# Conv ahead of the carried products, one ring of 4 KB tiles, and stores behind the loads, in a retention layer with a gated unit

## The chip, the core and the metric

The kernel runs on one core of a Trainium2 chip. The metric is device time in microseconds (us), from one launch of the whole kernel. TensorE (PE) does the matrix products and writes PSUM; VectorE (DVE), ScalarE (ACT) and GpSimd (POOL) do the elementwise work; SyncE (SP) issues nearly all DMAs. Each engine runs its own instructions in the order in which they were issued to it, and they wait for each other by semaphores.

## What is computed

Multi-head retention (causal, with a decay per head), its heads put side by side as `x`, then a gated unit: a causal convolution of 5 taps per channel through a sigmoid, times a product of `x` with a matrix, times another matrix. Cut to what matters:

```python
batch, n_heads, seq, head_dim = (8, 8, 576, 64)      # d_model 512, all float32

scores = scale * np.matmul(q, k.transpose(0, 1, 3, 2))
Dmat = np.where(rel >= 0, gamma[:, None, None] ** rel[None, :, :], 0.0)
x = np.matmul(scores * Dmat[None], v)                 # then heads side by side: (8, 576, 512)

for k in range(5):
    gate_pre += conv_w[k][None, None, :] * xp[:, k:k + S, :]
gate = 1.0 / (1.0 + np.exp(-gate_pre))
out = gate * (x @ w_val) @ w_out
```

## The kernel before, in words

**Units.** The sequence of each of the 8 batches is cut into two chunks of 256 positions and a tail of 64. A full unit is one chunk of one batch (units 0 to 15; an even unit is the first chunk of its batch, an odd one the second). Units 16 and 17 are the tails of four batches each. Within a unit two blocks of 128 positions are worked on side by side.

**Steps of a unit.** `load_half` brings half of the heads of k, q or v into a float32 tile of 2 KB per partition (`load1` brings all heads at once for the units in `whole`). Where it is given an engine as `touch`, that engine writes one element of the tile first, so that the load is not issued before that point of the engine's order. `cast_half` and `cast1` make bf16 of them, most on GpSimd; v is scaled by the decay on the way. `turn_bank` transposes half of k and q on TensorE into PSUM and copies it out on ScalarE (`kq`, L320). `scores` multiplies q and k, `masks` puts the causal mask on it on VectorE (L361, L365). `update` multiplies k and v for the running state and copies it to `xf` on ScalarE (L470); `states` sums it on GpSimd into `s1` and `s2` (L484 to L496). `carried(u, odd)` multiplies q with the state of the blocks before: the first thing in an output bank. It needs `s1` of its own unit and, for an odd unit, `s2` of the unit before. `values` adds the masked scores times v to the same bank. `fence` and `fence_first` read one element of the bank, so that what comes next into it waits for the first products there. `take_x` scales the bank and writes it to `xg` on VectorE (L436; L443 for tails).

**Steps of a job.** A job is one or two units of the gated unit. `conv` does the five taps as products with diagonal blocks (PSUM tile `a`) and ScalarE makes the gate from it (L542). `value` multiplies `xg` with the value weights, `gated` multiplies with the gate on VectorE (L565), `project` multiplies with the output weights, and ScalarE copies the result to `ob` (L580). `store` sends it out from SyncE.

**Tiles.** Units 0, 1, 16 and 17 are loaded whole into tiles of 4 KB with two buffers for each of k, q, v; the output weights have four constant tiles `wof`; the outputs have three buffers `ob` of 4 KB. PSUM: tile `a` (one buffer of two banks), `s` (the same), `o0` and `o1`, and two of `v`.

**Order.** The whole order is written out by hand (the tile scheduler is set to manual): a first phase for units 0 to 3 with their jobs (L619 to L774), a loop `for n in range(4, NU - 2)` (n = 4 to 15), and an end for units 16 and 17 (L813 to L854). The loop runs several things at once: carried, scores(n,1) and values of unit n; scores(n+1,0) and update of n+1; transposes of n+1 and n+2; loads of n+2 and n+3; casts of n+2 and n+3; conv, gate and gated product of an earlier job; project and store of unit n-3. `fill` adds small products with zeros until a count of products has a certain remainder. In n = 4 and 5 conv works on one of the older, half-wide jobs.

The loop's order, by its lines: carried and scores(n,1) (L782, L783), masks, fence on ScalarE (L785), conv (L786), the second half of k of n+2 (L787), scores(n+1,0) (L788), values(n,0), update with the states (L791), q (L792), values(n,1), first transposes (L795), gated products and loads of n+3 (L796 to L801), casts on GpSimd (L802 to L807), second transposes (L808), project and store (L810 to L812).

Of the kernel before, what the change touches and what calls it, by code (L numbers as in the profile page):

```python
# [13 lines left out]
F32 = mybir.dt.float32  # L14
# [7 lines left out]
def kernel(  # L22
# [10 lines left out]
    nc = tc.nc  # L33
# [8 lines left out]
    GB = 4  # L42
# [38 lines left out]
    with tc.manual_schedule():  # L81

        loaded = {}
        SRC = {"k": k, "q": q, "v": v}

        whole = (0, 1, NU - 2, NU - 1)
        HH = H // 2

        def load1(n, u, touch=None):
            kind, b, c = units[u]  # L90
            src = SRC[n]
            if u in whole:
                t = ldp.tile([P, H, 2 * D], F32, name=f"w{n}c")
                if touch:
                    touch(t[0:1, 0, 0:1], lsc[0:1])
                if kind == "full":
                    nc.sync.dma_start(out=t, in_=src[b, :, c * W:(c + 1) * W, :].rearrange("h (p r) d -> p h (r d)", r=2))
                else:
                    for i in range(GB):
                        nc.sync.dma_start(out=t[i * 32:(i + 1) * 32],  # L100
                                          in_=src[b + i, :, NC2 * W:S, :].rearrange("h (p r) d -> p h (r d)", r=2))
                loaded[n, u] = [(t, 0, H)]
            else:
                for i in range(2):
                    load_half(n, u, i)

        def load_half(n, u, i, touch=None):
            if u in whole:
                if i == 0:
                    load1(n, u, touch)  # L110
                return
            kind, b, c = units[u]
            t = ldp.tile([P, HH, 2 * D], F32, name=f"f{n}{i}")
            if touch:
                touch(t[0:1, 0, 0:1], lsc[0:1])  # L115
            nc.sync.dma_start(out=t, in_=SRC[n][b, i * HH:(i + 1) * HH, c * W:(c + 1) * W, :].rearrange("h (p r) d -> p h (r d)", r=2))
            loaded.setdefault((n, u), []).append((t, i * HH, HH))

        def load(u):
# [5 lines left out]
        cwn = consts.tile([KC * NP, P], F32, name="cwn")  # L125
        nc.scalar.dma_start(out=cwn, in_=moe_conv_w.rearrange("k (o i) -> (k o) i", i=P))
        wvf = [None] * NP
        wof = [consts.tile([P, DM], F32, name=f"wof{o}") for o in range(NP)]
        load(1)


# [4 lines left out]
            nc.sync.dma_start(out=wvf[g], in_=moe_w_val[:, g * P:(g + 1) * P].rearrange("(o i) j -> i o j", i=P))  # L136

        def load_wo(o, touch=None):
            if touch:
                touch(wof[o][0:1, 0:1], lsc[0:1])  # L140
            blk = 2 * (o % 2) + o // 2
            nc.sync.dma_start(out=wof[o], in_=moe_w_out[blk * P:(blk + 1) * P, :])
# [11 lines left out]

        def fill():
            z = ps_v.tile([P, 512], F32, name="v")
            while (made[0] + 32 + 16 + 16) % BLOCK != PLACE:
                matmul(z[:, 0:64], lhsT=zero[:, 0:P], rhs=zero[:, 0:64], start=True, stop=True)

        zero = consts.tile([P, 512], BF16, name="zero")  # L160
# [138 lines left out]
        def new_turned(u):  # L299
            if u not in kqt:  # L300
                kqt[u] = [tp_sb.tile([P, 2, 2, 2, 2, 64], BF16, name=f"kq{hf}") for hf in range(2)]
# [11 lines left out]
        def turn_bank(u, hf, ps):  # L313
            for i in range(2):
                for prl in range(2):
                    for r in range(2):
                        h = 2 * (2 * hf + prl)
                        transpose(ps[:, i, prl, r, :], bf[u]["kq"[i]][:, r, h:h + 2, :].rearrange("p h d -> p (h d)"), ident)
            new_turned(u)
            nc.scalar.copy(kqt[u][hf].rearrange("p i l r c a -> p (i l r c a)"), ps.rearrange("p i l r a -> p (i l r a)"))  # L320

        def turn_halves(*pairs, pool=None):
            if len(pairs) == 1 and pool is None:
                turn_bank(*pairs[0], ps_v.tile([P, 2, 2, 2, P], BF16, name="v"))
            else:
                ps = ps_a.tile([P, 2, 2, 2, 2, P], BF16, name="a")
                for (at, pair) in enumerate(pairs):
                    turn_bank(*pair, ps[:, at])

        def take_part(u, i, eng):  # L330
            for hf in range(2):
# [146 lines left out]

        def states(u):
            kind, b, cu = units[u]  # L480
            xf = xfs[u]
            s1 = stp.tile([P, NP, 64], BF16, name="s1")
            if cu == 0:
                nc.gpsimd.tensor_copy(s1, xf[:, 0])  # L484
                run = stp.tile([P, NP, 64], F32, name="run")
                nc.gpsimd.tensor_tensor(run, xf[:, 0], xf[:, 1], op=ALU.add)
                s2 = stp.tile([P, NP, 64], BF16, name="s2")
                nc.gpsimd.tensor_copy(s2, run)
                state[b, 0] = None
                state[b, "run"] = run  # L490
            else:
                mid = stp.tile([P, NP, 64], F32, name="mid")
                nc.gpsimd.tensor_tensor(mid, state[b, "run"], xf[:, 0], op=ALU.add)
                nc.gpsimd.tensor_copy(s1, mid)
                s2 = stp.tile([P, NP, 64], BF16, name=f"s4{b}", bufs=1)
                nc.gpsimd.tensor_tensor(s2, mid, xf[:, 1], op=ALU.add)  # L496
            state[b, 2 * cu + 1] = s1
            state[b, 2 * cu + 2] = s2
# [70 lines left out]
        def project(j, m, r, split=0, eng=None, pool=None):  # L569
            u = jobs[j][m]  # L570
            o = (pool or ps_v).tile([P, DM], F32, name="v" if pool is None else "s" if pool is ps_s else "o0")
            for jj in range(NP):
                z = zsb[j][:, jj, m * W:(m + 1) * W].rearrange("p (a r) -> p r a", r=2)
                n = DM // 2 if jj < split else DM
                for c in range(0, DM, n):
                    matmul(o[:, c:c + n], lhsT=z[:, r, :], rhs=wob[:, jj, c:c + n], start=(jj == 0 and c == 0),
                                     stop=(jj == NP - 1), skip_group_check=True)
            if r == 0:
                outs[u] = op_sb.tile([P, 2, DM], F32, name="ob")
            (eng or nc.scalar.copy)(outs[u][:, r], o)  # L580

        def last_rows(j):
# [9 lines left out]
            for r in range(2):  # L592
                (act, dve)[r](ob[r], o[r])  # L593
                for i in range(GB):
                    (nc.sync, nc.scalar)[i % 2].dma_start(out=out[b + i, NC2 * W:S, :].rearrange("(p r) n -> r p n", r=2)[r],
                                                          in_=ob[r][i * 32:(i + 1) * 32])

        def store(u):
            kind, b, c = units[u]
# [148 lines left out]
        carried(3, 0)  # L748
        scores(3, 1, lambda: carried(3, 1), pool=ps_a)
        masks(3, 1)  # L750
        load_half("k", 6, 0, dve)
        load_half("q", 6, 0)
        project(0, 0, 0)
        project(0, 0, 1)
        store(0)
        turn_halves((4, 0))
        values(3, 1)
        values(3, 0)
        cast_half("k", 5, 0)
        cast_half("q", 5, 0)  # L760
        fill()
        update(4)
        take_x(3)
        load_half("v", 6, 0, dve)
        turn_halves((4, 1), (5, 0))
        scores(4, 0)
        masks(4, 0)
        prep_tail_mask()
        cast1("v", 5)
        cast_half("k", 5, 1)  # L770
        cast_half("q", 5, 1)
        cast_half("k", 6, 0)
        cast_half("q", 6, 0)
        load_half("v", 6, 1)  # L774
        for n in range(4, NU - 2):
            def bring(name, u, i, eng):
                if u < NU:
                    load_half(name, u, i, eng)

            j, i = (HALVED, n - 4) if n < 6 else place[n - 2 - n % 2][0:1] + (n % 2,)  # L780
            jp, mp = place[n - 3]
            carried(n, 0)  # L782
            scores(n, 1, lambda: carried(n, 1))  # L783
            masks(n, 1)
            fence_first(n, act)  # L785
            conv(j, i)  # L786
            bring("k", n + 2, 1, act)  # L787
            scores(n + 1, 0, pool=ps_v)  # L788
            masks(n + 1, 0)
            values(n, 0)  # L790
            update(n + 1)  # L791
            bring("q", n + 2, 1, act)  # L792
            values(n, 1)
            turns = ps_a.tile([P, 2, 2, 2, 2, P], BF16, name="a")
            turn_bank(n + 1, 1, turns[:, 0])  # L795
# [6 lines left out]
            cast1("v", n + 2)  # L802
            cast_half("k", n + 2, 1)
            cast_half("q", n + 2, 1)
            if n + 3 < NU:
                cast_half("k", n + 3, 0)
                cast_half("q", n + 3, 0)  # L807
# [1 line left out]
            bring("v", n + 3, 1, act)  # L809
            project(jp, mp, 0)  # L810
            project(jp, mp, 1)
            store(n - 3)  # L812
        n = NU - 2  # L813
        j = place[n - 1][0]

        def rows_out(u, pools):
            for r in range(2):
                project(*place[u], r, pool=pools[r])
            store(u)

        carried(n, 0)
        scores(n, 1, lambda: carried(n, 1))
# [12 lines left out]
        scores(n + 1, 1, lambda: carried(n + 1, 1), pool=ps_a)  # L835
        masks(n + 1, 1)
        conv(j, 1, pool=ps_s)
        values(n + 1, 1)
        values(n + 1, 0)
        take_x(n + 1)  # L840
        value(j, 1, 0)
        value(j, 1, 1)
        conv(LAST - 1, 0)
        gated(j, 1, 0)
        gated(j, 1, 1)
        rows_out(n - 2, (ps_s, ps_o))
        gate_values(LAST - 1, 0, 0)
        gate_values(LAST - 1, 0, 1)
        conv(LAST, 0)
# [35 lines left out]
```

## Time and profile before

| | |
|---|---|
| median of 3 runs | 167.01 us (165.39 to 170.68) |
| the profiled execution | 166.65 us, span 164.9 us |
| granted TensorE clock, mean | 0.987 |
| busy: PE, DVE, ACT, POOL | 144.5, 104.9, 97.7, 104.2 us |
| moved by DMA | 40.32 MB: 30.42 read from HBM, 9.44 written to it |
| busy share of the DMA engines by stretches of 10 us, from 50 to 130 | 0.87 to 0.96 |
| the same from 130 to 140, 140 to 150 | 0.28, 0.13 |

The profile is of one execution. Its span runs from the first instruction to the last; what the time has beyond it lies around the program. A group or a line gives an engine, the line of the kernel (a helper's line, L150, for all matrix products), output and input tile, how many instructions, and how long. What stands in square brackets is how long the engine was idle ahead of it and what ended that. "SPq" is the DMA queue of SyncE; "us to landing" runs from the issue of a DMA to its last byte. The clock is the share of full speed that TensorE was granted.

By the granted clock and the chain of waits, the kernel has a first phase to about 41 us, the loop to about 133 us, and an end.

### The profile page before, as it was taken

Reading aid. Unit: us, or ns where it says so; the run is one execution under the profiler, and the core shown is the slowest. Engines: PE = TensorE matmul, PEld = TensorE weight load, DVE = VectorE, ACT = ScalarE, POOL = GpSimd, SP = SyncE. Lnnn points to the kernel's source line nnn. Section 1 sums busy time; section 2 is a strip of 40 time slices with the busy share of each in tenths; the row PEclk is TensorE's granted clock in tenths of the full one; section 3 lists DMA queues with packets and bytes.
Section 4 is the critical chain, followed back from the end, with each engine's and each line's share of the span. In section 5 each row is a group of like instructions: output and inputs, shape, how many; then the busy total and the mean of one; then the engine's idle time right before and its main releaser. Section 6 shows DMA issues by size and latency. Waiting matters only on the chain.

```text
span 164.9 us, 7223 instructions
## 1 busy us (share of the span) xinstructions
PE 144.5 (88%) x3038; PEld 99.6 (60%) x3058; DVE 104.9 (64%) x219; ACT 97.7 (59%) x176; POOL 104.2 (63%) x164
## 2 busy tenths in 40 slices
PE   6987899994998989999999999999987799799970
PEld 2456678873966757575866767575746455457530
DVE  5886877774658666676676768676666538633130
ACT  6894685975475756666666567666554264313620
POOL 7677869698797957979788887878276370000000
PEclk9999999999599999999999999999999999999999
DMA  4999999999779997999999898998898830303254
GB/s 131 347 346 343 322 303 319 323 280 341 217 214 302 279 299 208 310 281 289 292 274 309 245 323 231 319 274 279 218 286 237 251 132 10 131 0 127 109 161 115
DMA packets 62750, 40.32 MB, mean 244 GB/s; under 512 B 2410, under 2 KB 59774, under 8 KB 62718
## 3 DMA queue, kind: packets, MB, share of 16 engines
q1 hardware_dynamic: 62496, 39.59, 78.5%
q8 instruction: 24, 0.39, 1.0%
q10 hardware_dynamic: 222, 0.27, 0.6%
q14 instruction: 8, 0.07, 0.1%
HBM read 30.42 MB, written 9.44 MB: 242 GB/s over the span
## 4 chain that ended last, share of the span: by engine, by line
PE 54%; ACT 6%; DMA 6%; DVE 4%; issue 2%; SPq 1%; POOL 0%; ACTq 0%; POOLq 0%
PE v L150 25%; PE a L150 18%; PE o L150 6%; PE s L150 5%; ACT gate L542 5%; DMA out_dram<-ob 3%; DMA wqc<-in_q_dram 3%; DVE p L365 2%; ACT kq L320 1%; DVE xg L443 1%; SPq L100 1%; DVE p L361 1%; DVE last L593 0%; POOL qb L278 0%; ACTq L542 0%
## 5 line engine op out<-in xcount | busy, mean ns | idle before, releaser
L320 ACT COPY kq<-a 128x1024 bf16<-128x1024 bf16 x27 | 27.3, 1013 | 22.0 <-PE a L150 20.3
L150 PE MATMUL v<-xg,wvb 128*128 128x256 bf16 (+1 forms) x180 | 34.2, 322 | 1.9 <-DVE xg L443 1.2
L365 DVE TENSOR_TENSOR p<-s,mask 128x1024 bf16<-128x1024 f32 x17 | 20.8, 1223 | 15.5 <-PE s L150 15.5
L271 POOL TENSOR_TENSOR vb<-fv,gin 128x512 bf16<-128x512 f32 x28 | 28.7, 1044 | 1.1 <-PE a L150 0.9
L542 ACT ACTIVATE gate<-a 128x1024 f32<-128x1024 f32 (+1 forms) x17 | 16.6, 974 | 21.4 <-PE a L150 21.4
L565 DVE TENSOR_TENSOR zz<-gate,v 128x512 bf16<-128x512 f32 x24 | 16.5, 688 | 15.7 <-PE v L150 14.0
L150 PEld LDWEIGHTS <-wvb 128*128 128x128 bf16 x192 | 17.7, 97 | 12.5 <-issue 1.9
L150 PE MATMUL a<-xg,dg 64*64 64x256 bf16 (+1 forms) x460 | 23.7, 326 | 0.5 <-DVE xg L436 0.3
L436 DVE TENSOR_TENSOR xg<-o,gout 128x512 bf16<-128x512 f32 x32 | 22.2, 733 | 2.5 <-PE o L150 2.4
L150 PEld LDWEIGHTS <-kb 64*64 64x64 bf16 (+1 forms) x656 | 16.4, 108 | 11.8 <-issue 4.6
L278 POOL CAST kb<-fk 128x512 bf16<-128x512 f32 x28 | 17.1, 614 | 5.8 <-DMA fk<-in_k_dram 4.8
L150 PEld LDWEIGHTS <-kq 64*64 64x64 bf16 x576 | 17.1, 107 | 3.3 <-issue 2.7
L150 PE MATMUL v<-wob,zz 128*128 128x512 bf16 x79 | 18.8, 379 | 0.1
L150 PEld LDWEIGHTS <-dg 64*64 64x64 bf16 x480 | 17.3, 107 | 2.0 <-issue 1.2
L580 ACT COPY ob<-v 128x512 f32<-128x512 f32 x28 | 16.3, 582 | 2.2 <-PE v L150 1.3
L150 PE MATMUL o<-p,vb 64*64 64x128 bf16 x576 | 16.1, 222 | 1.1 <-DVE p L365 0.6
L361 DVE TENSOR_TENSOR p<-v,mask 128x512 bf16<-128x512 f32 x24 | 15.4, 685 | 0.8
L278 POOL CAST qb<-fq 128x512 bf16<-128x512 f32 x22 | 13.5, 616 | 3.3 <-DMA fq<-in_q_dram 1.6
L150 PE MATMUL a<-ident,kb 128*128 128x128 bf16 x108 | 10.7, 222 | 4.9 <-ACT gate L542 2.2
L150 PEld LDWEIGHTS <-zz 128*128 128x128 bf16 x96 | 8.8, 98 | 8.9 <-DVE fq L115 0.5
L150 PEld LDWEIGHTS <-vb 64*64 64x64 bf16 x576 | 11.8, 108 | 2.7 <-issue 2.2
L150 PE MATMUL s<-kq 64*64 64x128 bf16 x304 | 11.7, 222 | 1.5 <-DVE p L365 1.1
(111 smaller groups left out, 223.8 us busy)
## 6 DMA issues: line engine op xcount, KB each, us to landing
out_dram<-ob SPq DMA_DIRECT2D x16, 512.0 KB, 5.0
fk<-in_k_dram SPq DMA_DIRECT2D x28, 256.0 KB, 4.3
fq<-in_q_dram SPq DMA_DIRECT2D x28, 256.0 KB, 4.5
fv<-in_v_dram SPq DMA_DIRECT2D x28, 256.0 KB, 4.5
wkc<-in_k_dram SPq DMA_DIRECT2D x2, 512.0 KB, 4.9
wqc<-in_q_dram SPq DMA_DIRECT2D x2, 512.0 KB, 5.4
wvc<-in_v_dram SPq DMA_DIRECT2D x2, 512.0 KB, 5.9
wof<-in_moe_w_out_dram SPq DMA_DIRECT2D x4, 256.0 KB, 4.7
```

Of the source, the lines that this page charges most:

```text
L100: nc.sync.dma_start(out=t[i * 32:(i + 1) * 32], in_=src[b + i, :, NC2 * W:S, :].rearrange("h (p r) d -> p h (r d)", r=2))
L150: return f(*a, **k)
L271: nc.gpsimd.tensor_tensor(b[n][:, hs].rearrange("p h r d -> p (h r) d"), f.rearrange("p h (r d) -> p (h r) d", r=2), gin[:, units[u][2], h ...
L278: (eng or nc.gpsimd.tensor_copy)(b[n][:, :, hs].rearrange("p r h d -> p h r d"), f.rearrange("p h (r d) -> p h r d", r=2))
L320: nc.scalar.copy(kqt[u][hf].rearrange("p i l r c a -> p (i l r c a)"), ps.rearrange("p i l r a -> p (i l r a)"))
L361: nc.vector.tensor_tensor(p[:, par].rearrange("p l r a -> p l (r a)"), sps[u, hf][par].rearrange("p l r a -> p l (r a)"), mrow.to_broadcas ...
L365: nc.vector.tensor_tensor(p.rearrange("p e l r a -> p (e l) (r a)"), sps[u, hf].rearrange("p e l r a -> p (e l) (r a)"), mrow.to_broadcast ...
L436: nc.vector.tensor_tensor(x[:, b, :, PAD + i0:PAD + i0 + P].rearrange("p o (a r) -> p o r a", r=2), o[c].rearrange("p o (r a) -> p o r a", ...
L443: nc.vector.tensor_tensor(x[:, b + 2 * c + i, :, PAD + i0:PAD + S].rearrange("p o (a r) -> p o r a", r=2), o[c].rearrange("p o (r a) -> p ...
L542: nc.scalar.activation(t, cps[j, i], AF.Sigmoid)
L565: nc.vector.tensor_tensor(zsb[j][:, 2 * e + ss[0]:2 * e + ss[-1] + 1, :], gsb[j, i][e], vps[j, i, e], op=ALU.mult)
L580: (eng or nc.scalar.copy)(outs[u][:, r], o)
```

## The change

- `big()` gives tiles of 4 KB from one ring of eleven. Whole loads (units 0 and 1 only), pairs of output weights, and the outputs come from it in this order. Units 16 and 17 are loaded in halves, so each half is four DMAs of 64 KB where a whole load was four of 128 KB.
- `turn_halves` transposes all its pairs, then copies them out.
- In the loop conv comes ahead of carried (but in n = 4 behind it); the fence goes from ScalarE to VectorE; update comes ahead of values(n,0); the states of n+1 are made on GpSimd behind the casts of v, k and q of n+2. scores(n,1) no longer has a part of carried between its products.
- Outputs are put on a list. One store is issued at the end of each odd n, and the others by twos behind the loop.
- The entry of the loop and the end have a new order.

```diff
+        def big():
+            return ldp.tile([P, 2, DM], F32, name="big", bufs=11)
...
-        whole = (0, 1, NU - 2, NU - 1)
+        whole = (0, 1)
...
-                t = ldp.tile([P, H, 2 * D], F32, name=f"w{n}c")
...
+                t = big().rearrange("p c (h d) -> p (c h) d", d=2 * D)
+                nc.sync.dma_start(out=t, in_=src[b, :, c * W:(c + 1) * W, :].rearrange("h (p r) d -> p h (r d)", r=2))
...
+            hs = slice(i * HH, (i + 1) * HH)
+            if kind == "full":
+                nc.sync.dma_start(out=t, in_=SRC[n][b, hs, c * W:(c + 1) * W, :].rearrange("h (p r) d -> p h (r d)", r=2))
+            else:
+                for g in range(GB):
+                    nc.sync.dma_start(out=t[g * 32:(g + 1) * 32],
+                                      in_=SRC[n][b + g, hs, NC2 * W:S, :].rearrange("h (p r) d -> p h (r d)", r=2))
...
-        wof = [consts.tile([P, DM], F32, name=f"wof{o}") for o in range(NP)]
+        wof = [None] * NP
...
         def load_wo(o, touch=None):
+            if wof[o] is None:
+                t = big()
+                for c in range(2):
+                    wof[o // 2 * 2 + c] = t[:, c]
...
-            while (made[0] + 32 + 16 + 16) % BLOCK != PLACE:
+            while (made[0] + 32 + 16 + 8) % BLOCK != PLACE:
...
                 for (at, pair) in enumerate(pairs):
-                    turn_bank(*pair, ps[:, at])
+                    turn_bank(*pair, ps[:, at], take=False)
+                for (at, pair) in enumerate(pairs):
+                    take_bank(*pair, ps[:, at])
...
-                outs[u] = op_sb.tile([P, 2, DM], F32, name="ob")
+                outs[u] = big()
...
+        waiting = []
+
+        def stores(n):
+            for u in waiting[:n]:
+                store(u)
+            del waiting[:n]
...
         masks(3, 1)
+        prep_tail_mask()
...
-        store(0)
-        turn_halves((4, 0))
+        waiting.append(0)
+        turn_halves((4, 0), (4, 1))
...
         fill()
-        update(4)
+        update(4, now=False)
         take_x(3)
         load_half("v", 6, 0, dve)
-        turn_halves((4, 1), (5, 0))
-        scores(4, 0)
-        masks(4, 0)
-        prep_tail_mask()
         cast1("v", 5)
         cast_half("k", 5, 1)
         cast_half("q", 5, 1)
+        scores(4, 0, pool=ps_v)
+        masks(4, 0)
+        turn_halves((5, 0), pool=ps_a)
+        load_half("v", 6, 1, act)
+        states(4)
         cast_half("k", 6, 0)
         cast_half("q", 6, 0)
-        load_half("v", 6, 1)
+        def carry(n):
+            carried(n, 0)
+            carried(n, 1)
...
-            carried(n, 0)
-            scores(n, 1, lambda: carried(n, 1))
+            scores(n, 1)
             masks(n, 1)
-            fence_first(n, act)
+            if n == 4:
+                carry(n)
             conv(j, i)
+            if n > 4:
+                carry(n)
+            fence_first(n, dve)
             bring("k", n + 2, 1, act)
             scores(n + 1, 0, pool=ps_v)
             masks(n + 1, 0)
+            update(n + 1, now=False)
+            bring("q", n + 2, 1, act)
             values(n, 0)
-            update(n + 1)
-            bring("q", n + 2, 1, act)
             values(n, 1)
...
             cast1("v", n + 2)
             cast_half("k", n + 2, 1)
             cast_half("q", n + 2, 1)
+            states(n + 1)
             if n + 3 < NU:
                 cast_half("k", n + 3, 0)
                 cast_half("q", n + 3, 0)
...
-            store(n - 3)
+            waiting.append(n - 3)
+            if n % 2:
+                stores(1)
         n = NU - 2
+        stores(2)
...
-            store(u)
+            waiting.append(u)
+            stores(2)
...
         conv(j, 1, pool=ps_s)
+        value(j, 1, 0)
         values(n + 1, 1)
         values(n + 1, 0)
-        take_x(n + 1)
-        value(j, 1, 0)
+        gated(j, 1, 0)
         value(j, 1, 1)
         conv(LAST - 1, 0)
-        gated(j, 1, 0)
         gated(j, 1, 1)
-        rows_out(n - 2, (ps_s, ps_o))
+        take_x(n + 1)
+        stores(2)
+        rows_out(n - 2, (ps_s, None))
```

More of the change, by code (lines that the diff above doesn't have):

```diff
@@ L92, in load1 @@
             if u in whole:
-                t = ldp.tile([P, H, 2 * D], F32, name=f"w{n}c")
[L94 to L101, printed above, removed]
+                t = big().rearrange("p c (h d) -> p (c h) d", d=2 * D)
+                nc.sync.dma_start(out=t, in_=src[b, :, c * W:(c + 1) * W, :].rearrange("h (p r) d -> p h (r d)", r=2))
                 loaded[n, u] = [(t, 0, H)]
@@ L115, in load_half @@
                 touch(t[0:1, 0, 0:1], lsc[0:1])
-            nc.sync.dma_start(out=t, in_=SRC[n][b, i * HH:(i + 1) * HH, c * W:(c + 1) * W, :].rearrange("h (p r) d -> p h (r d)", r=2))
+            hs = slice(i * HH, (i + 1) * HH)
[5 more added lines that the diff above has]
+                                      in_=SRC[n][b + g, hs, NC2 * W:S, :].rearrange("h (p r) d -> p h (r d)", r=2))
             loaded.setdefault((n, u), []).append((t, i * HH, HH))
@@ L311, in turn, with turn_bank @@
                         transpose(ps[:, hf, prl, r, :], bf[u]["kq"[i]][:, r, h:h + 2, :].rearrange("p h d -> p (h d)"), ident)
-        def turn_bank(u, hf, ps):
+        def turn_bank(u, hf, ps, take=True):
             for i in range(2):
@@ L318, in turn_bank, with take_bank @@
                         transpose(ps[:, i, prl, r, :], bf[u]["kq"[i]][:, r, h:h + 2, :].rearrange("p h d -> p (h d)"), ident)
+            if take:
+                take_bank(u, hf, ps)
+        def take_bank(u, hf, ps):
             new_turned(u)
@@ L480, in states @@
             kind, b, cu = units[u]
+            if kind != "full":
+                return
             xf = xfs[u]
```

## The prediction

> **What bounds the kernel now.** I read the page first: TensorE is busy 88% of the span, no other engine above 64%, DMA at 0.9 and more through the middle. Next the chain of waits in order of time. One iteration of the steady loop (n = 10) and the start of the next:
>
> ```profile
> 87.46 1.03 ACT gate L542
> 88.54 0.61 PE a L150 x8
> 89.15 0.22 PE v L150
> 89.41 1.46 PE v L150 x6
> 90.87 0.45 PE a L150 x8
> 91.32 1.73 PE v L150 x8
> 93.05 0.24 PE o L150 x4
> ...
> 93.84 1.12 PE a L150 x17
> 95.03 1.03 ACT gate L542
> ```
>
> Columns are start, duration, what. The loop is TensorE all round, except one hop: conv ends, ScalarE makes the gate for 1.03, and the transposes into the same PSUM tile wait for it. Call G the start of a gate. G is 56.99, 65.14, 72.51, 80.09, 87.46, 95.03, 102.40, 109.98, 117.35, 125.93, 135.44 for n = 6 to 16: 7.38 where the unit has one carried state, 7.57 where it has two; 8.15, 8.58 and 9.51 once each.
>
> Then the timeline of GpSimd in the same iteration, and the DMA issues:
>
> ```profile
> 89.11 0.72 POOL L493 TENSOR_TENSOR mid<-run,xf 128x256 f32<-128x256 f32 x1 [0.28 <-ACT xf L470]
> 89.90 0.40 POOL L494 CAST s<-mid 128x256 bf16<-128x256 f32 x1
> 90.26 0.73 POOL L496 TENSOR_TENSOR s<-mid,xf 128x256 bf16<-128x256 f32 x1
> 90.94 2.05 POOL L271 TENSOR_TENSOR vb<-fv,gin 128x512 bf16<-128x512 f32 x2
> 92.93 0.62 POOL L278 CAST kb<-fk 128x512 bf16<-128x512 f32 x1
> 93.53 0.62 POOL L278 CAST qb<-fq 128x512 bf16<-128x512 f32 x1
> ```
>
> ```profile
> fk<-in_k_dram SPq DMA_DIRECT2D x1, 256.0 KB, 4.0
> fq<-in_q_dram SPq DMA_DIRECT2D x1, 256.0 KB, 4.3
> ...
> fk<-in_k_dram SPq DMA_DIRECT2D x1, 256.0 KB, 2.9
> fq<-in_q_dram SPq DMA_DIRECT2D x1, 256.0 KB, 3.3
> ```
>
> The states are made right after xf and are ready by G+3.5; carried needs them at G+5.5. The casts stand behind them. The last column of the issues is us to landing: 4.0 and 4.3 for the pair of 88.58 and 89.16, with a store of 512 KB issued 2 us ahead of it; 2.9 and 3.3 for the pair of 45.97 and 46.45, with little ahead.
>
> Last, TensorE's own waits at the entry of the loop and near the end, and the clock by stages (column before the last two):
>
> ```profile
> 38.46 0.38 PE L150 MATMUL a<-ident,kb 128*128 128x128 bf16 x4 [1.14 <-ACT kq L320]
> 40.74 0.25 PE L150 MATMUL s<-kq 64*64 64x128 bf16 x4 [1.11 <-DVE p L365]
> ...
> 142.43 0.64 PE L150 MATMUL o<-p,vb 64*64 64x128 bf16 x32 [0.26 <-DVE p L365]
> 144.64 0.38 PE L150 MATMUL v<-xg,wvb 128*128 128x512 bf16 x1 [1.25 <-DVE xg L443]
> ```
>
> ```profile
> 42.00:43.00 1.00, 1.00 (x46) 1.00 (x39) 0.90 (x2) 0.55 (x2) 1.00 (x3) 0.50 0.95 286
> 43.00:44.00 1.00, 1.00 (x51) 0.86 (x46) 1.00 (x2) 0.33 (x3) 0.34 (x1) 0.50 0.31 92
> ```
>
> Two waits within 2.5 us are followed by 3.3 us at about half clock (41.4 to 44.7).
>
> The sum below is against the profiled execution: 166.65 with a span of 164.9, so 1.75 outside it, which I keep. The median of the three runs is 167.01, 0.36 above it.
>
> **Entry (to conv of n = 6).** The change takes the two waits of 1.14 and 1.11 away: both banks of unit 4 are transposed before they are copied, and scores(4,0) uses another PSUM tile. But on GpSimd states(4) now stand behind v 2.04, k 0.61 and q 0.61 of unit 5. The cast before them ends at 37.15, so s is ready at 37.15 + 3.26 + 0.40 = 40.8 at best. TensorE, ready by my count at 38.95, waits 1.9 in carried(4), and conv(4) starts at 41.25 to 41.7 instead of 41.05. That much idling should bring the half clock again. In n = 4 I gain 0.3 (carried(5) leaves the front of conv(5)), in n = 5 the same plus the 0.35 that TensorE waits at 50.49 for a mask. Sum: +0.4 - 0.3 - 0.6 = **-0.5**; +0.5 if v(5) lands late, -2.0 if the half clock stays away (3.3 us at half speed cost about 1.5).
>
> **Steady loop (G of n = 6 to 13, 52.99 now).** Before conv there were 0.52 of carried and scores together (one state) or 0.71 (two). Afterwards scores alone, about 0.28, stand there, and carried alone, two diagonal quadrants at a time, about 0.45, fills the gap in which TensorE waits for the gate. After conv: 0.45 + 1.08 (scores, update, two values: 87.06 to 88.14) = 1.53, against 1.48 from the same point to the end of the gate at 88.54. So the period becomes 7.38 - 0.24 or 7.57 - 0.43, about 7.15. The extra 8.15 holds 0.42 in which TensorE waited for nothing the profile shows; I keep that. 7 x 7.15 + 0.42 = 50.5: -2.5. The fence goes from ScalarE (0.15) to VectorE, where masks(n+1,0) and the gated products queue behind it. It comes out at about G+0.6, before scores(n+1,0) give the mask anything to do, so I cost it at nothing; if that cover went, it would cost its 0.15 per iteration.
>
> What can eat this is the states. They are now queued behind v, k and q of unit n+2, and this q is issued at G+1.70, behind xf. It lands at G+1.70+L; then 0.65 for its cast, and 0.45 (first unit of a batch) or 1.25 (second) to s. Carried now needs s at G+7.15-0.40 = G+6.75. TensorE is in order: scores, update, values and all that follows wait behind it. So there is a stall when L exceeds 3.95 or 3.15. The rows give 2.9 to 4.5, and 6.0 and 6.5 once each (n = 6, 13). A store goes out ahead of the pair only in every second iteration now; 1.83 MB per iteration stand for 2.09. I take 3.3, the row with a lighter queue: 0.1 per second unit, 0.4 in all. **-2.1**, between -2.5 and +4.5 (the slower rival below).
>
> **Loads of the tail units (G of 13 to 16, 25.46 now).** Halves make 48 issues of 64 KB from 24 of 128 KB. SyncE took 0.45 to 0.47 for each of the latter, 0.41 for stores of 128 KB to 32 partitions; I take 0.42. Sixteen go out from G+3.42, then a store, then the eight of k and q of unit 16: the last at 13.5; with 2.5 to land (between 1.7 for 64 KB at the end and 2.8) 16.0. Then cast, mid and s: 17.9. Carried(15) could have run at 7.15 + 6.75 = 13.9, so TensorE idles 4.0. From there 7.7 of matmuls to G of n = 16: 25.6. So +0.1, and part of a half-clock stage, +0.6: **+0.7**, between -1 and +4 (0.47 an issue, 3.5 to land, the whole clock loss).
>
> The Trainium skill ("DMA: Bandwidth & Descriptors", Rules for kernel authors) says to coalesce small transfers, as at 64 KB and less most of the time is overhead. It speaks against these halves. By its fit of 2.0 us plus bytes over 436 GB/s, an estimate for 64 KB is 2.15 to land, and the stage would come 0.35 earlier than mine: issue time, not landing, decides.
>
> On the clock the row above is all I need. The same skill ("TensorE: Matmul & The Clock Gate", What's actually happening) has half clock after an idle window of some 3.4 us; the trace has it after two waits of about 1.1. By that rule the stall of 4.0 costs a whole half-clock stage, about 0.9 more than I counted.
>
> **End.** value(j,1,0) ahead of the last values, and take_x(17) behind both gated products, remove 0.26 and 1.25: **-1.5**. The deferred stores (about seven more of 512 KB) go into a stage with DMA shares of 0.1 to 0.4; the last ones could add up to 1.0 by queueing, taken as nothing because two stores land every 5 us or so against 2.6 for one. The ring of 4 KB tiles, whole loads and weights cost nothing: every slot's last reader is many us gone, and the output of unit 11 is the first to need a slot from a store (unit 0, issued in n = 5).
>
> Sum: -0.5 - 2.1 + 0.7 - 1.5 = -3.4: 163.25.
>
> **Rivals.** *Nothing much.* Stores were hidden anyway: SyncE waited 24.3 for outputs, but most of it behind the last load. If L stays at 4.0, each second unit stalls 0.85 (four times, 3.4, against 0.4): -3.4 + 3.0 = -0.4, 166.2. Against it: DMA has 12% less to move. For it: v, v, store still go out just before k and q every second time.
>
> *Slower: the states come too late.* If q lands as late as now, G+6.1 to 6.4 (casts at 93.53 and 86.54), s is ready at G+7.35 or G+8.15 and TensorE stalls 0.6 or 1.4, about 1.0 a time: 7 x 1.0 - 2.5 = +4.5 in the loop. With the tail loads near their upper price (+3.3: 0.47 an issue and the whole clock loss) and the other terms as above: -0.5 + 4.5 + 3.3 - 1.5 = +5.8, 172.4. It decides from a mean stall of about 0.5, where the -3.4 is used up. For it: the two landings of 6.0 and 6.5, harmless now, would hit TensorE directly.
>
> **How the numbers follow.** Forecast 0.42 (own range 160.5 to 164.5), nothing much 0.28, late states 0.30. Of the first, a little is above 163.7, the bound of 2%, which is about what a measurement of this kernel can tell from no change; of the second a little is below it. So faster 0.43, within 0.25, slower 0.32. The range must reach into the slow case: 160 to 171.5. Predicted 163.3.
>
> **What would show it.** Right: gates 7.1 to 7.3 apart; no wait of TensorE on s in the loop beyond 0.2; the transposes no longer waiting for the gate; one wait of about 4 ahead of carried(15), ended by GpSimd; the 1.25 near the end gone. Wrong: waits of TensorE or its weight loads ended by the s writes (L484, L494) in every second iteration; k and q landing later than G+5.2; a second stage at half clock before the end; the last store landing over 1 us behind the last row.

## The result, and the profile after

The changed kernel takes 177.43 us (median of 4 runs, 176.41 to 178.05); the kernel before, with one more run beside it, 166.59 (165.39 to 170.68). The ratio is 1.067, 95% interval 1.058 to 1.076: slower. Some executions of a kernel take over 1.5% longer than its fastest one, mostly at a lower clock: medians and ranges here are over all executions, ratios without these. The profiled execution took 177.21 with a span of 175.4, so 1.8 outside it, as before.

The starts of the gates, G, divide the span again. G(n) is the gate of iteration n:

| stage | before | after | difference | predicted |
|---|---|---|---|---|
| start to G(6) | 56.99 | 56.18 | -0.81 | -0.5 |
| G(6) to G(13) | 52.99 | 57.64 | +4.65 | -2.1 (the slower rival +4.5) |
| G(13) to G(16) | 25.46 | 33.73 | +8.27 | +0.7 (the slower rival +3.3, upper bound +4) |
| G(16) to the end | 29.46 | 27.85 | -1.61 | -1.5 |

The two outer stages went as forecast. In the loop G is 56.18, 63.30, 72.25, 79.36, 88.15, 95.26, 106.71, 113.82: every other period is 7.11 to 7.12, shorter than the 7.38 of before, and the others are 8.95, 8.79 and 11.45. The share of the chain of waits by engine says where to look (part 4 of the page; before, it had PE 54%, DMA 6% and POOL 0%):

```profile
PE 38%; DMA 27%; POOL 12%; DVE 7%; SPq 6%; issue 5%; ACT 1%; POOLq 0%; DVEq 0%; ACTq 0%
```

The program's end now hangs on loads and on GpSimd for 39% of the span. Which, the view of waits names. Columns are engine, output, line, what it waited for, us in total, times, longest; lines between are left out.

```profile
PE o L157 <- POOL s L509: 16.2, 7, 7.6
...
POOL qb L285 <- DMA fq<-in_q_dram: 12.2, 12, 2.1
...
POOL kb L285 <- DMA fk<-in_k_dram: 9.7, 10, 1.9
```

L509 is the first state of an odd unit (L494 before). TensorE waits for it seven times: the carried products of every odd unit from 5 to 13, 1.3 to 2.7 each, and once 7.65 ahead of carried(15); the seventh is 0.2 or less. In the page of before this wait does not appear. The chain of waits shows how one of them comes about, in iteration 10 (G = 88.15):

```profile
89.44 0.43 POOL qb L285
89.87 6.00 DMA fq<-in_q_dram
...
95.99 0.61 POOL qb L285
96.61 0.68 POOL mid L508
...
97.38 0.38 POOL s L509
...
97.80 0.31 PE o L157
```

Read it backwards. TensorE's first carried product of unit 11 starts at 97.80, when `s` is written; `s` waits for `mid`, `mid` for the cast of q of unit 12 ahead of it in GpSimd's order, and that cast for a DMA issued at 89.87, G+1.72, that took 6.00. Nothing in unit 11 needs q of unit 12; only the order of one engine ties them. The same stretch in the timeline of GpSimd, with its idle time in brackets:

```profile
93.88 0.61 POOL L285 CAST kb<-fk 128x512 bf16<-128x512 f32 x1 [1.48 <-DMA fk<-in_k_dram]
95.99 0.61 POOL L285 CAST qb<-fq 128x512 bf16<-128x512 f32 x1 [1.50 <-DMA fq<-in_q_dram]
96.57 0.72 POOL L508 TENSOR_TENSOR mid<-run,xf 128x256 f32<-128x256 f32 x1
```

Before, `mid` and `s` stood ahead of these casts (89.11 and 89.90) and GpSimd waited for q without anyone waiting for GpSimd.

Then the stage of the tail loads: first SyncE's issues, where a count of 4 or 8 gives the time of them all, then TensorE in iteration 9, the cast of q of unit 16, and TensorE at the end of the wait:

```profile
119.19 1.76 SPq L118 DMA_DIRECT2D fk<-in_k_dram  x4
121.05 2.95 SPq L118 DMA_DIRECT2D fq<-in_q_dram  x4
124.09 5.15 SPq L118 DMA_DIRECT2D fv<-in_v_dram  x8
...
129.82 2.16 SPq L118 DMA_DIRECT2D fk<-in_k_dram  x4
132.10 1.86 SPq L118 DMA_DIRECT2D fq<-in_q_dram  x4
```

```profile
80.57 0.52 PE L157 MATMUL o<-kq,s 64*64 64x128 bf16 x12 [1.31 <-POOL s L509]
...
136.11 0.61 POOL L285 CAST qb<-fq 128x512 bf16<-128x512 f32 x1 [1.50 <-DMA fq<-in_q_dram]
137.92 0.85 PE L157 MATMUL o<-kq,s 64*64 64x128 bf16 x12 [7.65 <-POOL s L509]
```

The issues begin at G(13)+5.4 and take 14.8, some 0.6 each. The last q of unit 16 is issued by 134.0, its cast starts at 136.11, `s` is ready behind it, and carried(15) goes at 137.92. The same twelve products took 0.52 at 80.57 and take 0.85 here, because the clock has gone down (columns of the windows: length, then busy us and count of PE, PEld, DVE, ACT, POOL, then granted clock, DMA share and GB/s):

```profile
134.00:138.00 4.00, 0.08 (x2) 0.08 (x4) 0.00 (x0) 0.00 (x0) 2.43 (x5) 0.62 0.54 138
138.00:142.00 4.00, 3.83 (x74) 3.30 (x76) 1.45 (x3) 0.63 (x1) 2.15 (x4) 0.52 0.55 135
```

### The profile page after: what moved, and what is told of

It reads as the page before. It is cut to its first block, busy times and chain, and to the rows that moved or that the text cites. A ratio compares the mean times of both kernels' runs of the same rounds, so it can differ in the third digit from the quotient of the medians.

```text
span 175.4 us, 7267 instructions
## 1 busy us (share of the span) xinstructions
PE 145.0 (83%) x3038; PEld 94.3 (54%) x3058; DVE 106.7 (61%) x232; ACT 96.8 (55%) x171; POOL 104.1 (59%) x166
## 4 chain that ended last, share of the span: by engine, by line
PE 38%; DMA 27%; POOL 12%; DVE 7%; SPq 6%; issue 5%; ACT 1%; POOLq 0%; DVEq 0%; ACTq 0%
PE v L157 16%; DMA fq<-in_q_dram 16%; PE o L157 9%; PE a L157 8%; SPq L118 6%; DMA fk<-in_k_dram 5%; PE s L157 5%; POOL qb L285 4%; DMA fv<-in_v_dram 3%; DMA big<-in_q_dram 3%; DVE p L378 3%; POOL mid L508 2%; POOL vb L278 2%; POOL kb L285 2%; DVE xg L449 1%
## 5 line engine op out<-in xcount | busy, mean ns | idle before, releaser
L278 POOL TENSOR_TENSOR vb<-fv,gin 128x512 bf16<-128x512 f32 x32 | 32.8, 1042 | 12.0 <-DMA fv<-in_v_dram 10.2
L285 POOL CAST kb<-fk 128x512 bf16<-128x512 f32 x32 | 19.4, 610 | 11.5 <-DMA fk<-in_k_dram 9.7
L157 PE MATMUL o<-kq,s 64*64 64x128 bf16 (+1 forms) x256 | 11.0, 225 | 18.2 <-POOL s L509 16.2
L285 POOL CAST qb<-fq 128x512 bf16<-128x512 f32 x26 | 15.9, 613 | 12.7 <-DMA fq<-in_q_dram 12.2
L157 PEld LDWEIGHTS <-s 64*64 64x64 bf16 x256 | 8.5, 114 | 23.6 <-POOL s L509 19.1
L595 ACT COPY big<-v 128x512 f32<-128x512 f32 x29 | 16.8, 580 | 2.2 <-PE v L157 1.1
L157 PEld LDWEIGHTS <-kq 64*64 64x64 bf16 x576 | 12.4, 108 | 6.6 <-issue 6.4
L157 PEld LDWEIGHTS <-dg 64*64 64x64 bf16 x480 | 13.1, 106 | 4.8 <-issue 1.0
L157 PE MATMUL o<-p,vb 64*64 64x128 bf16 x576 | 13.3, 229 | 0.8 <-DVE big L147 0.4
L483 ACT COPY xf<-s 128x512 f32<-128x512 f32 x14 | 8.1, 581 | 10.1 <-POOL kb L285 6.6
```

The source lines that it names most:

```text
L157: return f(*a, **k)
L278: nc.gpsimd.tensor_tensor(b[n][:, hs].rearrange("p h r d -> p (h r) d"), f.rearrange("p h (r d) -> p (h r) d", r=2), gin[:, units[u][2], h ...
L285: (eng or nc.gpsimd.tensor_copy)(b[n][:, :, hs].rearrange("p r h d -> p h r d"), f.rearrange("p h (r d) -> p h r d", r=2))
L483: nc.scalar.copy(xf.rearrange("p c o d -> p c (o d)"), xyt[:, :, 0:NP * 64])
```

## The experiments

The theory after this reading: the states, put behind the casts of k and q, make carried wait for DMA landings, and that one part of the change costs more than all others gain. Rivals: the deferred stores or the halves of the tails cost it, or carried behind conv is itself late. Each profile was taken apart at the same gates:

| run | median, us | ratio to before (95%) | to G(6) | loop | G(13) to G(16) | end |
|---|---|---|---|---|---|---|
| e1 states early | 167.19 | 1.002 (0.997-1.007) | 58.59 | 50.29 | 28.45 | 28.77 |
| e3 states behind v | 166.59 | 1.005 (1.001-1.009) | 55.60 | 50.30 | 28.99 | 28.51 |
| e5 before, states late | 184.78 | 1.116 (1.109-1.124) | 58.51 | 64.69 | 30.64 | 29.46 |
| e2 states(15) early | 175.25 | 1.057 (1.044-1.070) | 56.09 | 56.19 | 31.79 | 28.23 |
| e8 all states early | 166.29 | 1.003 (0.999-1.007) | 57.91 | 50.29 | 28.64 | 28.66 |
| e4 before, conv first | 165.36 | 1.001 (0.996-1.005) | 56.10 | 51.71 | 25.25 | 29.44 |
| e12 before, tail halves | 171.30 | 1.039 (1.032-1.046) | 57.27 | 52.43 | 29.15 | 31.05 |
| e7 e8, whole tails | 162.01 | 0.980 (0.972-0.988) | 55.70 | 51.15 | 26.00 | 27.75 |
| e9 before, order and end | 161.96 | 0.979 (0.973-0.986) | 56.88 | 50.30 | 25.75 | 27.87 |
| e11 e9, new entry | 163.53 | 0.981 (0.970-0.992) | 54.80 | 50.49 | 25.53 | 27.88 |
| e10 store in even n | 170.61 | 1.034 (1.028-1.041) | 55.38 | 54.00 | 31.53 | 27.89 |
| e6 a store in each n | 174.42 | 1.056 (1.051-1.062) | 57.48 | 55.43 | 31.37 | 28.52 |

(The kernel before took 165.39 beside e1, e3, e4, e5, 165.65 beside e2, e7, e8, e9, and 165.18 beside the others. For e7, e9 and e11 the interval is clear of no change, but reaches to both sides of 2%.)

### Is it the place of the states?

**e1**, the changed kernel with the loop's states made right behind `xf` again, all else as changed:

```diff
-            update(n + 1, now=False)
+            update(n + 1)
...
-            states(n + 1)
```

> The changed kernel, but in the loop the states of n+1 are made right behind update(n+1), ahead of the casts of v, k and q. Theory (late states: carried waits for s, which stands on GpSimd behind casts that wait for k and q): gates 7.1 to 7.3 apart in n = 6 to 13, no wait of TensorE on s, the waits of 1.3 to 2.7 gone; carried(15) no longer waits 7.65, but the transposes of unit 16 then wait some 2 to 5 for the tail loads; 165 us, between 162.5 and 168. Rival A (the tail loads in halves and the moved stores cost the time, the states are only where it shows): little gain, 174 or more, the gates of every second iteration still 8.8 or more apart. Rival B (carried behind conv costs by itself): the same as A in the loop.

**e3**, only past k and q, and still behind v:

```diff
             cast1("v", n + 2)
+            states(n + 1)
             cast_half("k", n + 2, 1)
             cast_half("q", n + 2, 1)
-            states(n + 1)
```

> The changed kernel, but the states of n+1 stand behind the cast of v only, ahead of those of k and q. Theory, in its narrow form (it is the landing of k and q that counts, not GpSimd's work in front): s is ready about 4.5 + 1.2 = 5.7 behind the gate, carried needs it at 6.75, so no waits in the loop and about the time of the run with early states, 165 within 1.5 either way. If GpSimd's work in front counts: waits of about half, 169 to 173. Rival A or B: 174 or more.

**e5**, the kernel before with nothing changed but that its states go behind the casts of v, k and q:

```diff
-            update(n + 1)
+            update(n + 1, now=False)
...
             cast_half("q", n + 2, 1)
+            states(n + 1)
...
         def states(u):
             kind, b, cu = units[u]
+            if kind != "full":
+                return
```

> The kernel before with only this changed: in the loop the states stand behind the casts of v, k and q. Theory: s comes 7.3 to 8.2 behind the gate and carried, still the first thing of the iteration, needs it at 5.5: a wait of 1.9 to 2.6 in each of 12 iterations and more in the last: 187 to 195. Rival A: at most 3 over the kernel before, 170 or less.

Moving the states alone brings the changed kernel from 177.4 to about 167, and putting them late, with nothing else changed, costs the kernel before 19 us. In e1 and e3 the periods from G(6) to G(13) are 7.11 to 7.28, and the loop takes 50.3: the forecast's 50.5. In e3 the first states of odd units still stand behind 2.17 of GpSimd's work on v, and TensorE waits for them only ahead of carried(15), 2.57. So it is not GpSimd's work on v that hurts but the wait for k and q, whose casts take only 0.6 each. In e5 the loop took 11.7 more than before. Its waits:

```profile
PE o L150 <- POOL s L496: 12.0, 6, 5.3
...
PE o L150 <- POOL s L486: 3.5, 4, 1.0
```

In the kernel before, carried stands at the front of the iteration, so the slack is smaller and the late states cost more, in even units (L486) too. e5 came out a little under what I expected (187 to 195).

**e2**, only states(15) early, to split the tail stage:

```diff
-            update(n + 1, now=False)
+            update(n + 1, now=n == NU - 4)
...
-            states(n + 1)
+            if n != NU - 4:
+                states(n + 1)
```

> The changed kernel, but in n = 14 alone the states of unit 15 are made right behind update(15), ahead of the casts of unit 16. Theory: carried(15) no longer waits 7.65; TensorE then waits for the transposes of unit 16, whose k and q are cast at about 23 behind the gate of n = 13 as in the changed kernel, so the gate of n = 16 comes some 3.5 earlier and all of the loop up to n = 13 stays as slow as it was: 174, between 172.5 and 175.5. If all that the tail stage lost (8.3) were the states' place: 169.

The 7.65 ahead of carried(15) went, and the stage became 1.9 shorter, not 7.65: the transposes of unit 16 now wait for the same loads, 2.8 for `kb` and 2.2 for `qb`. A wait at the head of a queue is worth only what the next one leaves.

**e8**, e1 with states(4) right behind update(4) as well, for the 3.3 us for which e1 waits at the entry:

```diff
-        update(4, now=False)
+        update(4)
...
-        states(4)
```

> The changed kernel with every states call right behind its update, in the entry too (states(4)). Theory: against the run with the loop's states early, the wait of 2 to 3.3 ahead of carried(4) goes, and with it the half clock behind it in the executions that had it: 164.5, between 163 and 166. Rival: the entry waits for v, k and q of unit 5 all the same and nothing is gained, 166.5 or more.

A miss: 166.29 where 164.5 was expected. The wait ahead of carried(4) is gone (0.16 for its weights), but update(5) then waits for the casts of unit 5, which now stand behind the states (0.39 for `vb`, 1.24 for `kb`), and the granted clock behind that is 0.60 from 44 to 48. This profile also came out of the first phase 1.4 late (its third gate at 28.18, for 26.82 in the changed kernel), where the edit plays no part. The entry has one chain through GpSimd, and the order only chooses who waits.

### What are the other parts worth?

**e4**, the kernel before with scores, conv, carried and a fence on VectorE in this order, and nothing else:

```diff
+            scores(n, 1)
+            masks(n, 1)
+            conv(j, i)
             carried(n, 0)
-            scores(n, 1, lambda: carried(n, 1))
-            masks(n, 1)
-            fence_first(n, act)
-            conv(j, i)
+            carried(n, 1)
+            fence_first(n, dve)
```

> The kernel before with only this changed: in the loop scores(n,1) without a part of carried between, then conv, then carried, then the fence on VectorE. Theory: the gap ahead of the transposes closes, gates 7.1 to 7.2 apart, 0.3 less in each of 8 to 11 iterations: 163 to 164.5. Rival B (carried behind conv costs): 166.6 or more.

A miss: no difference that can be told. The loop gained 1.28, not the forecast's 2.5; its periods are 7.26 and 7.50. **e9** adds update ahead of values(n,0), and the changed end:

```diff
+            update(n + 1)
+            bring("q", n + 2, 1, act)
             values(n, 0)
-            update(n + 1)
-            bring("q", n + 2, 1, act)
             values(n, 1)
```

> The kernel before, with its own tiles, loads and stores, but the loop's order on TensorE as changed (conv, carried, fence on VectorE, scores, update, both values; the states right behind update) and the changed order of the end. Theory: gates 7.1 and 7.3 apart as in the runs with early states, about 2.5 less over the loop, and 1.5 less in the end: 161.5, between 160 and 163.5. Rival (conv ahead of carried gives nothing, as in the run that had only that): 164 from the end alone.

The loop goes from 51.71 to 50.30, and the time to 161.96. So the forecast's 7.15 needs both. In e4 values(n,0) come almost right behind carried and meet the fence on VectorE: the chain of waits has the fence in it at 93.46 for 0.17, 0.24 with the gaps on both sides. In e9 update, some 0.5, stands between. That this is the whole difference is a reading; no run took the fence alone. In e9 the chain of waits has only TensorE for an iteration of 7.11 (gates at 85.68 and 92.79), and no line of another engine stands in it:

```profile
87.63 1.46 PE v L150 x6
89.09 0.45 PE a L150 x8
89.53 1.73 PE v L150 x8
91.26 0.35 PE s L150 x16
91.61 1.08 PE a L150 x20
92.69 0.33 PE o L150 x12
```

**e12**, the kernel before with only its tail units loaded in halves, 48 issues of 64 KB for 24 of 128 KB:

```diff
-        whole = (0, 1, NU - 2, NU - 1)
+        whole = (0, 1)
```

> The kernel before with only the loads of units 16 and 17 in halves (48 issues of 64 KB for 24 of 128 KB). Theory: the stage from the gate of n = 14 to that of n = 16 goes from 18.1 to about 21.4, as it did between the runs with early states with whole and with halved tails; nothing else changes: 168.5, between 167 and 170. Rival (in the kernel before other waits of that stage cover it): 166.5 or less.

**e7**, the opposite: e8 with the tails whole again, in tiles of the ring, and a store in every iteration from n = 10 on so that the ring has room:

```diff
-        whole = (0, 1)
+        whole = (0, 1, NU - 2, NU - 1)
...
-            if n % 2:
+            if n % 2 or n > 9:
```

> The same as the run with every states call early, but units 16 and 17 are loaded whole, 24 issues of 128 KB where there were 48 of 64 KB, into tiles of the ring; for that one store more is issued in n = 10, 12 and 14. Theory (the halves cost what the loop wins): the stage from the gate of n = 14 to that of n = 16 goes from about 21.5 to 18 as in the kernel before; 161, between 159.5 and 163. Rival (SyncE's issues are not what the stage waits for): within 1 of the run with every states call early.

The halves alone cost the kernel before 6 us, a miss (168.5 was expected, 170 at most): 3.7 between G(13) and G(16), where the transposes of unit 16 wait 2.84 for `kb` and 1.28 for `qb`, and 1.6 behind it, where those of unit 17 wait 1.27 for `qb`. Whole tails bring e8 4.3 us and make the first version that beats both kernels (its three added stores are part of that).

**e11**, e9 with the changed entry (both banks turned before they are copied, scores(4,0) in another tile, states(4) behind the casts of unit 5):

```diff
-        turn_halves((4, 0))
+        turn_halves((4, 0), (4, 1))
...
+        scores(4, 0, pool=ps_v)
...
+        states(4)
```

> The kernel before with the loop's order and the end of the run that had both (states right behind update, tails whole, its own tiles and a store in each iteration), and the changed entry of the loop besides (both banks of unit 4 turned before they are copied, scores(4,0) in another tile, states(4) behind the casts of unit 5, carried ahead of conv in n = 4). Theory: the two waits of 1.14 and 1.11 go, the wait for s of unit 4 comes; gate of n = 6 at about 56 for 56.9; 161.3, between 160.2 and 162.5. If the entry only trades one wait for another: 162 within 0.5.

A miss in the median: 161.3 was expected, 162.5 at most. Its profiled execution is the shortest (160.84, clock 0.997), and G(6) comes 2.1 earlier than in e9; its other three took 163 to 164. It can't be told apart from e9 and e7.

### Do the stores ahead of k and q matter?

**e10**, the changed kernel with the loop's store at the end of even n, not odd, and **e6**, with one in each:

```diff
-            if n % 2:
+            if n % 2 == 0:
                 stores(1)
```

> The changed kernel with its one store in the loop issued at the end of each even n instead of each odd n. It is open why only odd units stall: a store goes out just ahead of their k and q, and their s needs one more instruction (mid, 0.72 + 0.07) than that of an even unit. If the store ahead counts: the waits for s of odd units fall by about 1 (a store of 512 KB is 1.5 to 2 us of the queue), even units get waits of up to 0.5; 174.5, between 172.5 and 176.5. If only the extra instruction counts: the same pattern and 177.4 within 1.

```diff
-            if n % 2:
-                stores(1)
+            stores(2)
```

> The changed kernel with each store issued at the end of its own iteration, as in the kernel before; states still late. If the store ahead of k and q counts: odd units stall as in the changed kernel and even units by up to 0.5 more; 179, between 177.5 and 182. If the moved stores were what costs the time (they pile up behind the loads): faster than the changed kernel, 174 or less.

In the changed kernel the store goes out 2 us ahead of the q behind which the states of an odd unit stand. That iteration's issues (last column: us to landing):

```profile
out_dram<-big SPq DMA_DIRECT2D x1, 512.0 KB, 4.8
fv<-in_v_dram SPq DMA_DIRECT2D x1, 256.0 KB
fk<-in_k_dram SPq DMA_DIRECT2D x1, 256.0 KB, 4.5
fq<-in_q_dram SPq DMA_DIRECT2D x1, 256.0 KB, 6.0
```

With a store ahead this q took 4.8, 4.7 and 6.0 (n = 6, 8, 10). Without one it took 3.1, 2.8, 3.2 and 2.8 (n = 7, 9, 11, 13), but there it was also issued later, at G+3.2 to G+5.3, behind a stall. In e10 the stalls change sides. They come in the even units (up to 1.33), whose states are one step shorter, and the odd ones stay below 0.9 up to unit 13; ahead of carried(15) TensorE still waits 6.81:

```profile
71.47 0.31 PE L157 MATMUL o<-kq,s 64*64 64x128 bf16 x4 [1.33 <-POOL s L499]
...
94.42 0.52 PE L157 MATMUL o<-kq,s 64*64 64x128 bf16 x12 [0.86 <-POOL s L509]
```

The time falls by 6.8 for a shift of the store by one iteration, more than I expected. The landings carry a part of that account. In e10 k took 4.5 to 5.6 behind a store (issued at 64.08, 79.95, 94.78, 110.50) and 3.0 to 3.6 without one (71.36, 87.23, 103.12); q took 3.8 to 4.6 behind one (80.56, 96.44, 111.89) and 2.8 to 4.4 without (57.40, 73.27, 88.10), so for q the two overlap. The 0.8 of slack that even units have more is the other part that I can name; the two were not taken apart. The Trainium skill ("DMA: Bandwidth & Descriptors", Queues, rings and completion order) says that the descriptors of one queue are consumed in order on each DMA engine, which the rows of k fit and those of q leave open. e6 fits less well: with a store ahead of every pair it should by that reasoning have taken 179, and it took 174.42, 3 us less than the changed kernel. It stalls in odd and in even units, 14.7 in all against 18.2. That is near the 174 of its rival, that the deferred stores themselves cost time. Why not more is open; what the run shows is that deferring the stores was no gain in this order. Where the states are early the loop takes the same with the stores deferred (e1, e3 and e8, 50.3) and with one in each iteration (e9, 50.30).

## Why the prediction was wrong

**Slower was named, and forecast at 0.30.** The rival "the states come too late" had the mechanism, the place and the direction, and three of the four signs listed for it came: waits of TensorE ended by the `s` writes in every second iteration, q landing later than G+5.2 (q of 89.87 at G+7.7), a further stage at half clock. The fourth, a late last store, did not: the span ends 4.6 behind the last copy to `last`, before and after. e1, e3 and e5 show that it is the cause. The range ended at 171.5, below the 172.4 at which this rival was priced, so it left out the middle of a case that had a chance of 0.30.

**The step that failed: "I take 3.3, the row with a lighter queue"**, for L, the time to landing of the q that now stands ahead of the states. The formula around it held: a stall where L exceeds 3.15, for the second unit of a batch. With the measured L of 4.8, 4.7 and 6.0 it gives 1.65, 1.55 and 2.85; measured were 1.47, 1.31 and 2.65. Only L was wrong, and nearer rows were in the loop of before: there this q took 4.3 to 4.5 in five iterations, and 6.0 and 6.5 in n = 6 and 13; the 3.3 was from the entry. 4.0 and 4.3 was the pair with a store 2 us ahead, and every second iteration kept just that. I had argued that fewer bytes in total mean an earlier landing; in the iterations that mattered it came no earlier. From gate to gate the DMA engines were busy 0.90, 0.95, 0.98 and 0.94 in n = 6, 8, 10 and 12, and 0.50 to 0.65 in the odd ones between, so the bytes saved were saved where nothing waited for them. (The sum was loose too: 3.3 exceeds 3.15 by 0.15, not 0.1, and between G(6) and G(13) three odd units can stall, not four.) A late carried also delays the next unit's `xf`, on ScalarE, and the q issued behind it, to G+3.2 and later; no even unit stalled in the loop for that.

**The rival's +4.5 in the loop against +4.65 is partly chance.** It took seven stalls of about 1.0. There were three, 5.4 together, none in an even unit, and the rest is the clock: after the wait of 2.65 the granted clock was 0.5 for some 3 us, and the period came to 11.45, 1.65 more than 7.15 and the wait.

**The tail term, +0.7, was mis-sized**, and its upper bound of +4 too. It is the larger half of the miss: 7.6 us, where the loop's term missed by 6.8. I had s(15) ready at G(13)+17.9; it was +24.1. Of these 6.2, 2.0 are the first issue, at +5.4 and not +3.4, because carried(13) was itself late (in e1 and e8, with no such stall, it is at +3.6); the rest is the issues, about 0.6 each where I took 0.42 (0.47 as the bound). Among them, four took 1.76 at the start, 0.44 each, and eight of v 5.15. A whole stage at half clock added about 1.3 more than I counted. The view of before had long issues for the whole tails as well, and the reading of 0.45 to 0.47 left them out:

```profile
113.40 1.82 SPq L100 DMA_DIRECT2D wkc<-in_k_dram  x4
115.32 3.14 SPq L100 DMA_DIRECT2D wqc<-in_q_dram  x4
118.56 1.87 SPq L100 DMA_DIRECT2D wvc<-in_v_dram  x4
...
121.06 3.26 SPq L100 DMA_DIRECT2D wkc<-in_k_dram  x4
```

Two of these four groups took about 0.8 an issue. e8 gives the price with no late states: 28.64, +3.2 over before. So about 3.2 of the 8.3 are the halves, and 5.1 the late states.

On these halves the Trainium skill ("DMA: Bandwidth & Descriptors", Rules for kernel authors) had the right sign with its rule to coalesce, and I gave it no weight: e12 and e7 put the price of halving at 6.1 and 4.3 us. The 2.15 that I estimated for a landing was near: loads of 64 KB landed in 2.2 to 2.4 (medians), under the 2.5 of the sum. My remark that issue time decides, not landing, agrees with the rows: 24 issues took 14.8, and a landing is some 2 us behind the last of them. An issue costs the same for 64 KB as for 128 KB (0.45), so halves double the time of issuing.

**What held.** The period of 7.15 (7.11 and 7.28 where nothing waits). The entry (-0.5 forecast, -0.81) for a mixed reason: the wait ahead of carried(4) was 2.00 against 1.9, but the half clock that I expected there did not come in this profile. The end (-1.5, -1.61): the 1.25 is gone, and the deferred stores cost nothing that can be seen there. No wait for a free tile of the ring shows in the view of waits. **What held only in company:** the fence at nothing. That is so with update ahead of values (e9); e4, without it, lost half of the loop's gain.

**Where the gain went.** The order on TensorE and the end are worth about 2% by themselves (e9, 1.4 to 2.7%). The halves took this back (e8, 1.003), and the late states took a further 11 us.

## What to carry to other kernels

On an engine that works in order, whatever stands behind a cast that waits for a load inherits that load's landing: before putting a producer later in such a queue, list who waits for it, and cost it with the landing measured with the same things queued ahead, not with a mean. Judge a moved step by the slack of its consumer in each kind of iteration, since here the even units had slack and the odd ones had none. When a part is worth a few per cent, build it alone on the kernel before: two of the parts here were a gain and two a loss, and the sum told of neither.

## What the runs showed of the hardware

- The DMA engines were less busy in the mean (0.80 from 50 to 95, where before they had 0.87 and more in all stretches from 50 to 130), and yet loads of 256 KB behind a store took 4.5 to 6.0, no less than the 4.0 to 4.5 of most of the busier kernel before. In those iterations the share was 0.90 to 0.98, in the others 0.50 to 0.65. A mean share of busy time says little about one landing.
- Half clock came after waits of TensorE of 2.65 and 7.65, but not after one of 2.00 at the entry, where the kernel before had it after two of about 1.1. By the Trainium skill ("TensorE: Matmul & The Clock Gate", What's actually happening) it takes an idle window of some 3.4 us, in a window that runs freely; the long wait agrees, the 2.65 and the two of 1.1 are shorter than that.
- A DMA issue of SyncE takes 0.45 for 64 KB as for 128 KB in the shortest groups (four in 1.80 and in 1.82), and 0.74 to 0.82 in the longest (four in 2.95, of 128 KB in 3.14 and 3.26). What lengthens it is open.
